# Masked row maxima of an attention kernel: the unused sums go to a byte tile instead of back into PSUM

## The chip, the cores and the metric

The kernel runs on one core of a Trainium2 chip. The time is the device time of one execution in microseconds; before and after are compared by the median of several runs. One further execution was profiled, and all rows quoted are from that one.

A core has five engines with a queue of instructions each. TensorE (PE) multiplies matrices into PSUM, which is divided into banks of 128 x 512 floats; VectorE (DVE), ScalarE (ACT) and GpSimd (POOL) work on elements; SyncE (SP) issues most DMAs. An engine takes its instructions in order; where one waits for a semaphore, all that stand behind it on the queue wait too.

## The reference

Four layers with a residual: a linear attention with learned features (A), an attention over segments with a memory (B), A, B. The change lies in B. There, 2048 tokens of 512 features are cut into 4 segments of 512 tokens, and each of 32 heads of width 16 does a causal softmax inside its segment:

```python
for s in range(N):
    qs, ks, vs = q[:, :, s], k[:, :, s], v[:, :, s]
    logits = jnp.einsum("bhqd,bhkd->bhqk", qs, ks) * scale + mask
    p = _softmax(logits, axis=-1)
    a_dot = jnp.einsum("bhqk,bhkd->bhqd", p, vs)
    pq = phi(qs)
    num = jnp.einsum("bhld,bhde->bhle", pq, M)
    den = jnp.einsum("bhld,bhd->bhl", pq, z)[..., None] + 1e-6
    a_mem = num / den
    o = g * a_mem + (1.0 - g) * a_dot
    outs.append(o)
    pk = phi(ks)
    M = M + jnp.einsum("bhld,bhle->bhde", pk, vs)
    z = z + jnp.einsum("bhld->bhd", pk)
```

A softmax subtracts the maximum of each row of logits. These row maxima are what the changed instructions compute.

## The kernel before

A layer B goes over 32 items m: 4 segments times 4 groups of heads times 2 halves, four heads an item. An item takes five steps (R = 5) of one loop in `steps`, numbered k; a table written by hand (`FIRST`, `GAPS`, `LAST`, `FINAL`) says what else each step does. Each step of the loop issues, in this order, a part of `attend(m)`, a part of `maxima` for an item some steps ahead, and the work of the table.

`maxima(m)` computes the masked row maxima. PE multiplies blocks of queries (block i, 128 rows) with the keys up to that block, 128 (i + 1) columns, for two heads at a time (e = 0, 1), the first into PSUM bank mx, the second into bank my; there is one buffer of each. The list of rounds is such that a bank holds either one product of 512 columns, or two: 128 and 384 columns, or 256 and 256. So five rounds an item, three of them with two products in a bank. Then DVE takes each product's maxima in `top`: it adds the mask to the product, takes the maximum along the row into a column of the small tile mxs, and writes the masked sums, which nobody reads, back over the product. In the profile one such maximum is two instructions: CUSTOM_DVE_ANT_0, called a pass here, and DVE_READ_ACCUMULATOR2_ANT, which delivers the maximum. PE may fill a bank again when DVE's last read is done.

`put_maxima` has PE transpose the 16 columns, ACT copy them negated into the tile mt (MT buffers), and a DMA on ACT's queue put them as a row into the stacked queries, so that the next product for `attend` subtracts the maximum by itself. `attend(m)` multiplies the same blocks into the banks lg, ACT takes the exponential of all into a tile P, POOL sets the masked triangle to zero, and `weighted` multiplies P with the values into pv.

`close` and `read` call `invert`, which turns denominators around by DMA: `compact` loads them from den into the tile dn on SP's queue, `flip` takes the reciprocal on DVE one or two steps later, `put` stores dn as inv, `spread` copies it out wide, `load` brings that back. There are two buffers of dn; the tile holds 128 x 64 floats.

The order of the work on each engine is fixed: the wrapper `Ordered` and the function `held` tie each instruction of DVE, ACT, POOL, SP and PE behind the one that the code issued before it. What a framework adds are the waits: a semaphore wait wherever an instruction touches a tile, or a bank of PSUM, that another one writes or has written, also if both are on one engine.

The helper that records an instruction has line 163 (DVE, ACT, POOL, SP) or 185 and 189 (PE's matmuls and transposes); the rows are told apart by the tiles they name.

Of the kernel before, what the change touches and what calls it, by code (L numbers as in the profile page):

```python
# [18 lines left out]
P = 128  # L19
# [8 lines left out]
OT = 3  # L28
TA = 8
OO = 5  # L30
MT = 2
PV = 1
G = 3
R = 5
# [73 lines left out]
def interleave_kernel(ctx, tc, x_in, a_wqkv, a_wphi, a_wo, b_wq, b_wk, b_wv, b_wo, b_beta,  # L108
# [4 lines left out]
    cp = ctx.enter_context(tc.tile_pool(name="cp", bufs=1))  # L113
# [10 lines left out]
    def nm(s):  # L124
        uid[0] += 1
        return f"{s}_{uid[0]}"

    def T2(tag, bufs, dt=F32, shape=(P, 512)):
        return sp.tile(list(shape), dt, tag=tag, bufs=bufs, name=nm(tag))

    def PS(tag, bufs, shape=(P, 512)):
        return ps.tile(list(shape), F32, tag=tag, bufs=bufs, name=nm(tag))
# [49 lines left out]
    def mm(*a, **k):  # L182
        n = a[0].free_size()
        work[0] += n / 2.26 if k["rhs"].dtype == F32R else (n * 2 / 2.4 + 25 if "tile_position" in k else 2 * max(112, n * 2 / 2.4))
        return held(nc.tensor.matmul(*a, **k))  # L185

    def tp(*a):
        work[0] += 108
        return held(nc.tensor.transpose(*a))  # L189
# [7 lines left out]
    mask = cp.tile([P, 512], F32, name="mask")  # L197
# [2 lines left out]
    share = cp.tile([P, 8], F32, name="share")  # L200
    gated = cp.tile([P, NC, 4], F32, name="gated")
    ones = cp.tile([32, P], F32, name="ones")

    def constants():

        sync.dma_start(out=mask, in_=c_mask)
        sync.dma_start(out=eb, in_=b_beta.unsqueeze(0).broadcast_to([P, H]))
        yield
        yield
        act.activation(eb, eb, AF.Exp, scale=-1.0)  # L210
        dve.tensor_scalar(eb, eb, 1.0, None, op0=ADD)
        dve.reciprocal(gates[:, 1, :], eb)
        dve.tensor_scalar(gates[:, 0, :], gates[:, 1, :], -1.0, 1.0, op0=MUL, op1=ADD)
        for j in range(4):
            dve.tensor_copy(share[32 * j : 32 * j + 32, :], gates[32 * j : 32 * j + 32, 0, j:H:4])
        for hf, col in enumerate((24, 28)):
            dve.tensor_scalar(share[:, hf:8:2], share[:, hf:8:2], -1.0, bd[:, col : col + 1], op0=ADD, op1=MUL)
        dve.tensor_scalar(share, share, 1.0, None, op0=ADD)
        for f in range(2):
            rows = slice(64 * f, 64 * f + 64)  # L220
            dve.tensor_tensor(out=gated[rows], op=MUL,
                              in0=gates[rows, 1, :].rearrange("p (c f h) -> p c f h", c=NC, f=2)[:, :, f, :],
                              in1=bdB[rows].unsqueeze(1).broadcast_to([64, NC, 4]))
        dve.tensor_copy(ones, bd[0:32, 25:26].broadcast_to([32, P]))
# [7 lines left out]
    def dtile(shape, name):  # L232
        return dr.tile(list(shape), F32, name=name)
# [705 lines left out]
    class LayerB:  # L939
# [98 lines left out]
        def invert(self, s, c, k, parts):  # L1038


            lo, hi = 8 * parts[0], 8 * parts[-1] + 8
            n = (hi - lo) * 4
            tiles = {}

            def compact():
                d = tiles["d"] = T2("dn", 2, shape=(P, 64))
                sync.dma_start(out=d[:, 0:n], in_=self.den(s, c)[lo:hi].rearrange("h (x i) -> (h x) i", i=n))

            def flip():
                dve.reciprocal(tiles["d"][:, 0:n], tiles["d"][:, 0:n])  # L1050

            def put():
                tiles["i"] = dtile((hi - lo, D), nm("inv"))
                sync.dma_start(out=tiles["i"].rearrange("h (x i) -> (h x) i", i=n), in_=tiles["d"][:, 0:n])

            def spread():
                wide = tiles["w"] = dtile((hi - lo, DH, D), nm("wide"))
                sync.dma_start(out=wide, in_=tiles["i"].unsqueeze(1).broadcast_to([hi - lo, DH, D]))

            def load():  # L1060
                for i in parts:
                    t = self.inv[s, c, i] = T2(*(("mmq", 2) if i else ("KN", 1)))
                    sync.dma_start(out=t, in_=tiles["w"][8 * i - lo : 8 * i - lo + 8].rearrange("h d n -> (h d) n"))
            for j, f in zip((0, 1, 2, 3, 5) if s < NSEG - 1 else (0, 2, 3, 4, 6), (compact, flip, put, spread, load)):
                self.at(k + j, f)
# [84 lines left out]
        def maxima(self, m):  # L1150


            s, c, hf = m // 8, m % 8 // 2, m % 2
            Q, K = [t[:, 2 * hf : 2 * hf + 2, :] for t in self.st[s, c]["set"]]
            mx = T2("mxs", 2, shape=(P, 16))

            def prod(pb, r, i, at, w):
                for e in range(2):
                    q, k = Q[64 * e : 64 * e + 63, r, :], K[64 * e : 64 * e + 63, r, :]
                    mm(pb[e][:, at : at + w], lhsT=q[:, i * P : (i + 1) * P], rhs=k[:, 0:w],  # L1160
                       start=True, stop=True, tile_position=(64 * e, 0))

            def top(pb, e, r, i, at):
                n = (i + 1) * P
                col = (e * 2 + r) * 4 + i
                pl = pb[e][:, at : at + n]
                with tc.high_priority():
                    dve.tensor_tensor_reduce(
                        out=pl, in0=pl, in1=mask[:, 512 - n : 512], scale=1.0, scalar=-3.0e38,
                        op0=ADD, op1=MAX, accum_out=mx[:, col : col + 1])  # L1170

            for what in ([(0, 0, 0), (0, 2, P)], [(0, 3, 0)], [(1, 0, 0), (1, 2, P)],
                         [(0, 1, 0), (1, 1, 256)], [(1, 3, 0)]):
                pb = [PS(t, 1) for t in ("mx", "my")]
                for r, i, at in what:
                    prod(pb, r, i, at, max(256, (i + 1) * P))
                for e in range(2):
                    for r, i, at in what:
                        top(pb, e, r, i, at)
                self.mx[m] = mx  # L1180
                yield

        def put_maxima(self, m):
# [3 lines left out]
            tp(pt[0:16, 0:P], self.mx.pop(m), ident)  # L1187
            mt = T2("mt", MT, F32R, shape=(16, P))
            act.activation(mt, pt[0:16, 0:P], AF.Copy, scale=-1.0)
# [352 lines left out]
```

## Time and profile before

| | us |
|---|---|
| median of 3 runs before | 1481.35 |
| lowest of them | 1480.6 |
| the profiled execution | 1477.25 |
| its span, first to last instruction | 1475.5 |
| ACT busy | 810.8 |
| POOL busy | 731.6 |
| all reads of the accumulator on DVE, 1024 | 145.1 |
| the exponentials, ACT, 320 of 128x1024 | 328.6 |

The span is what the rows of the trace cover; the 1.75 us between it and the execution's time lie around it. Busy times are of instructions that work on data; time in which an engine waits is given as idle time before an instruction, with the instruction that ended it. The rows that matter for the change are quoted in the prediction.

### The profile page before, as it was taken

To read this page: it belongs to the slowest core of one execution; us is meant where nothing else is said; L and a number is where in the kernel's file an instruction comes from. 1 tells how busy PE (TensorE), PEld (TensorE's weight loads), DVE (VectorE), ACT (ScalarE), POOL (GpSimd) and SP (SyncE) were. 2 spreads that over 40 slices of the span, in tenths; PEclk is the share of its full clock that TensorE was granted. 3 is DMA by queue.
4 is the path that set the end of the run, shared out by engine and by line. 5 is a ranking of instruction groups with operands and counts; after the bars stand their busy time and mean duration, and the time that the engine had idled before them with its cause. 6 is when DMAs were issued, how large, how long until landed. Compare 5 with 4: busy or idle time off the path is not lost.

```text
span 1475.5 us, 32962 instructions
## 1 busy us (share of the span) xinstructions
PE 1395.7 (95%) x12052; PEld 960.0 (65%) x12052; DVE 1022.0 (69%) x3007; ACT 810.8 (55%) x1228; POOL 731.6 (50%) x1066
## 2 busy tenths in 40 slices
PE   7989999999999999998899999999999999999987
PEld 6778778765566566655567887886555565566544
DVE  4766877777667767677446677867776776766762
ACT  5546345446576576565534434543656766755652
POOL 1668754224455556454424456631345556645532
PEclk9999999999999999999999999999999999999998
DMA  5387375546556556567630105764565574565451
GB/s 189 115 293 245 114 245 166 164 133 176 155 145 202 167 147 200 161 182 195 205 129 32 50 30 183 220 184 116 152 178 140 148 235 141 153 203 162 121 187 44
DMA packets 139792, 236.33 MB, mean 160 GB/s; under 512 B 26576, under 2 KB 40016, under 8 KB 138864
## 3 DMA queue, kind: packets, MB, share of 16 engines
q1 hardware_dynamic: 138480, 233.70, 52.9%
q8 instruction: 97, 1.59, 0.5%
q10 hardware_dynamic: 1152, 0.52, 0.1%
q14 instruction: 63, 0.52, 0.1%
HBM read 129.17 MB, written 55.18 MB: 125 GB/s over the span
## 4 chain that ended last, share of the span: by engine, by line
PE 73%; DVE 10%; DMA 5%; ACT 5%; issue 3%; POOL 3%; SPq 1%; ACTq 0%; POOLq 0%; DVEq 0%
PE g L185 44%; PE pv L185 8%; PE lg L185 8%; PE mx L185 4%; PE g L189 4%; PE my L185 3%; DVE mx L163 2%; ACT P L163 2%; DMA dn<-den 2%; DVE my L163 2%; PE lg L189 1%; DVE es L163 1%; SPq L163 1%; POOL tmp L163 1%; POOL P L163 1%
## 5 line engine op out<-in xcount | busy, mean ns | idle before, releaser
L163 ACT ACTIVATE P<-lg 128x1024 f32<-128x1024 f32 x320 | 328.6, 1027 | 182.3 <-PE lg L185 168.9
L163 POOL TENSOR_SCALAR_AFFINE_SELECT P<-P 128x256 f32<-128x256 f32 (+1 forms) x448 | 190.2, 439 | 427.9 <-ACT P L163 421.6
L163 DVE CUSTOM_DVE_ANT_0 mx<-mx,mask 128x128 f32<-128x128 f32 (+3 forms) x512 | 254.8, 498 | 181.7 <-PE my L185 128.7
L163 DVE CUSTOM_DVE_ANT_0 my<-my,mask 128x128 f32<-128x128 f32 (+3 forms) x512 | 265.8, 519 | 6.5
L185 PE MATMUL lg<-e,e 64*128 64x256 f32 (+2 forms) x1024 | 170.5, 391 | 26.2 <-ACT P L163 26.1
L185 PE MATMUL g<-hh,wqk 128*128 128x512 f32 x512 | 185.0, 410 | 0.7 <-ACT mt L163 0.7
L185 PE MATMUL g<-w,oh 128*128 128x512 f32 x512 | 173.4, 420 | 2.4 <-ACT oh L163 2.4
L185 PE MATMUL pv<-P,v 128*32 128x512 f32 (+3 forms) x2048 | 168.4, 448 | 2.2 <-ACT ot L163 2.2
L185 PEld LDWEIGHTS lg<-e,e 64*128 64x128 f32 x1024 | 82.1, 186 | 126.5 <-issue 55.9
L185 PE MATMUL my<-e,e 63*128 63x256 f32 (+2 forms) x512 | 148.3, 350 | 12.5 <-DVE mxs L163 11.9
L185 PE MATMUL mx<-e,e 63*128 63x256 f32 (+2 forms) x512 | 146.6, 337 | 5.9 <-DVE mxs L163 5.8
L163 DVE DVE_READ_ACCUMULATOR2_ANT mxs<- 128x1 f32 x1024 | 145.1, 142 | 0.0
L185 PE MATMUL g<-w,hh 128*128 128x512 f32 x448 | 144.8, 404 | 0.0
L185 PEld LDWEIGHTS pv<-P,v 128*32 128x32 f32 x2048 | 54.5, 110 | 105.3 <-issue 92.4
L185 PEld LDWEIGHTS g<-hh,wqk 128*128 128x128 f32 x512 | 96.6, 189 | 31.6 <-issue 10.1
L185 PEld LDWEIGHTS g<-w,oh 128*128 128x128 f32 x512 | 90.7, 193 | 30.3 <-issue 11.0
L185 PEld LDWEIGHTS my<-e,e 63*128 63x128 f32 x512 | 84.6, 187 | 32.4 <-DVE mxs L163 11.2
L185 PE MATMUL g<-w,ol 128*128 128x512 f32 x256 | 103.9, 406 | 0.0
L185 PEld LDWEIGHTS mx<-e,e 63*128 63x128 f32 x512 | 90.7, 188 | 15.4 <-DVE mxs L163 5.1
L185 PE MATMUL g<-hl,wqk 128*128 128x512 f32 x256 | 100.6, 393 | 0.0
L185 PEld LDWEIGHTS g<-w,hh 128*128 128x128 f32 x448 | 81.6, 191 | 22.7 <-issue 6.1
L163 POOL TENSOR_TENSOR P<-P,es 128x512 f32<-128x512 f32 x32 | 49.0, 1531 | 85.9 <-DVE es L163 85.8
(156 smaller groups left out, 2682.7 us busy)
## 6 DMA issues: line engine op xcount, KB each, us to landing
e<-ta SPq DMA_DIRECT2D x384, 128.0 KB
wqk<-wqk SPq DMA_DIRECT2D x64, 512.0 KB
x<-x SPq DMA_DIRECT2D x48, 256.0 KB
wide<-inv SPq DMA_DIRECT2D x20, 512.0 KB
xr<-x SPq DMA_DIRECT2D x32, 256.0 KB
x<-xr SPq DMA_DIRECT2D x28, 256.0 KB
tmp<-U SPq DMA_DIRECT2D x56, 128.0 KB
KN<-wide SPq DMA_DIRECT2D x28, 256.0 KB
```

What stands on the lines that cost most here:

```text
L163: i = f(*a, **k)
L185: return held(nc.tensor.matmul(*a, **k))
L189: return held(nc.tensor.transpose(*a))
```

## The change

In rounds with two products in a bank the masked sums go to a new tile in SBUF, junk, of bytes: two slots of 384, slot 0 for the first product and slot 1 for the second, the same two for both banks. In rounds with one product they still go back into the bank. To keep SBUF's use as it was, mt (512 bytes a partition) and dn (256 bytes) go from two buffers to one: 768 bytes, as many as junk takes.

```diff
-MT = 2
+MT = 1
...
+    junk = cp.tile([P, 2, 384], mybir.dt.uint8, name="junk")
...
             def compact():
-                d = tiles["d"] = T2("dn", 2, shape=(P, 64))
+                d = tiles["d"] = T2("dn", 1, shape=(P, 64))
...
-            def top(pb, e, r, i, at):
+            def top(pb, e, r, i, at, spare):
                 n = (i + 1) * P
                 col = (e * 2 + r) * 4 + i
                 pl = pb[e][:, at : at + n]
                 with tc.high_priority():
                     dve.tensor_tensor_reduce(
-                        out=pl, in0=pl, in1=mask[:, 512 - n : 512], scale=1.0, scalar=-3.0e38,
+                        out=pl if spare is None else junk[:, spare, 0:n], in0=pl, in1=mask[:, 512 - n : 512], scale=1.0, scalar=-3.0e38,
                         op0=ADD, op1=MAX, accum_out=mx[:, col : col + 1])
...
                 for e in range(2):
-                    for r, i, at in what:
-                        top(pb, e, r, i, at)
+                    for j, (r, i, at) in enumerate(what):
+                        top(pb, e, r, i, at, j if len(what) > 1 else None)
```

## The prediction, made before the changed kernel ran

> **What bounds the kernel now.** I read the page's first part and the chain that ended last first, for the engine that sets the time.
>
> ```profile
> PE 1395.7 (95%) x12052; PEld 960.0 (65%) x12052; DVE 1022.0 (69%) x3007; ACT 810.8 (55%) x1228; POOL 731.6 (50%) x1066
> PE 73%; DVE 10%; DMA 5%; ACT 5%; issue 3%; POOL 3%; SPq 1%; ACTq 0%; POOLq 0%; DVEq 0%
> ```
>
> TensorE (PE) is busy for 95% of the span and holds 73% of the chain; VectorE (DVE), whose work is changed, holds 10%. Next, the view of busy times by stage, for 285 to 690 us and 1003 to 1400 us, in which the attention of the two layers runs steadily (x is a count):
>
> ```profile
> core 0: us, PE busy (x) PEld busy (x) DVE busy (x) ACT busy (x) POOL busy (x), PEclk, DMA share, GB/s
> sum 802.00, PE 769.62 PEld 475.80 DVE 580.44 ACT 498.42 POOL 404.03; mean PE 384.81 PEld 237.90 DVE 290.22 ACT 249.21 POOL 202.01
> ```
>
> In these 802 us PE idles for 802.00 - 769.62 = 32.4 us and DVE works 72% of the time. So no relief of DVE there can bring more than about 32 us, 2.2% of the span. What DVE itself costs PE is in the view of the column of maxima (mxs), under who waited for it:
>
> ```profile
> who waited for it (us, times):
>   PE my L185: 11.9, 29
> ...
>   PE mx L185: 5.8, 5
> ```
>
> 34 waits, 17.7 us: matmuls into the two shared banks that DVE had not yet released.
>
> **The change part by part.** *The wait between two maxima of one bank.* One round of four maxima in order of time, DVE's rows alone (start, duration, what):
>
> ```profile
> 1207.61 0.30 DVE L163 CUSTOM_DVE_ANT_0 mx<-mx,mask 128x128 f32<-128x128 f32 x1 [0.58 <-PE mx L185]
> 1207.83 0.14 DVE L163 DVE_READ_ACCUMULATOR2_ANT mxs<- 128x1 f32 x1
> 1208.00 0.57 DVE L163 CUSTOM_DVE_ANT_0 mx<-mx,mask 128x384 f32<-128x384 f32 x1
> 1208.49 0.14 DVE L163 DVE_READ_ACCUMULATOR2_ANT mxs<- 128x1 f32 x1
> 1208.49 0.33 DVE L163 CUSTOM_DVE_ANT_0 my<-my,mask 128x128 f32<-128x128 f32 x1
> 1208.73 0.14 DVE L163 DVE_READ_ACCUMULATOR2_ANT mxs<- 128x1 f32 x1
> 1208.91 0.57 DVE L163 CUSTOM_DVE_ANT_0 my<-my,mask 128x384 f32<-128x384 f32 x1
> 1209.39 0.14 DVE L163 DVE_READ_ACCUMULATOR2_ANT mxs<- 128x1 f32 x1
> ```
>
> Each maximum is a pass (CUSTOM) and a read of its accumulator. Where the bank changes, at 1208.49, the next pass starts together with the read. Where the bank stays, it starts 0.03 us after the read has ended (1208.00 against 1207.83 + 0.14), since it reads a bank that the first pass wrote. So the wait costs 0.39 - 0.22 = 0.17 us on mx and 0.42 - 0.24 = 0.18 on my. With sums going elsewhere, that dependence is gone. But a pass that starts under a read is longer, by the shapes kept apart:
>
> ```profile
> L163 DVE CUSTOM_DVE_ANT_0 my<-my,mask 128x256 f32<-128x256 f32 x128 | 57.5, 449 | 2.2
> L163 DVE CUSTOM_DVE_ANT_0 mx<-mx,mask 128x256 f32<-128x256 f32 x128 | 55.2, 431 | 42.7 <-PE my L185 27.3 <-PE mx L185 13.0
> L163 DVE CUSTOM_DVE_ANT_0 my<-my,mask 128x128 f32<-128x128 f32 x128 | 42.4, 331 | 0.0
> L163 DVE CUSTOM_DVE_ANT_0 mx<-mx,mask 128x128 f32<-128x128 f32 x128 | 37.9, 296 | 60.6 <-PE my L185 40.1 <-PE mx L185 19.5
> ```
>
> my at 128x128 always follows another bank's pass, mx mostly follows a pause: 331 against 296 ns, 0.03 us that the released pass pays. Net 0.14 us a pair. Pairs: the 256 passes of 128x128 each go with one of 128x384, the 256 of 128x256 go with each other, 128 pairs; 384 in all, 384 x 0.14 = 54 us of DVE time.
>
> On DVE's queue the 34 ns and the read are idle time of an engine that mostly has slack, so the path decides. By the 29 waits for my: one shared round holds two waits, 0.28 us of relief, and the mean wait is 11.9 / 29 = 0.41 us, so 29 x 0.28 = 8.1 us come back. One of them:
>
> ```profile
> 1166.81 0.57 DVE L163 CUSTOM_DVE_ANT_0 my<-my,mask 128x384 f32<-128x384 f32 x1
> 1167.29 0.14 DVE L163 DVE_READ_ACCUMULATOR2_ANT mxs<- 128x1 f32 x1
> 1167.58 0.35 PE L185 MATMUL my<-e,e 63*128 63x256 f32 x1 [0.54 <-DVE mxs L163]
> ```
>
> The five waits for mx hold the late DMA below, so I count nothing for them. By the chain instead: its shares are "DVE mx 2.1%" and "DVE my 1.6%", 3.7% of 1475.5 = 55 us, while all passes are busy for 254.8 + 265.8 = 520.6 us:
>
> ```profile
> by line: PE g L185 43.8%; PE pv L185 8.2%; PE lg L185 7.6%; PE mx L185 4.4%; PE g L189 3.7%; issue 3.3%; PE my L185 3.1%; DVE mx L163 2.1%; ACT P L163 1.8%; DMA dn<-den 1.8%; DVE my L163 1.6%; PE lg L189 1.4%; DVE es L163 1.2%; SPq L163 1.1
> L163 DVE CUSTOM_DVE_ANT_0 mx<-mx,mask 128x128 f32<-128x128 f32 (+3 forms) x512 | 254.8, 498 | 181.7 <-PE my L185 128.7
> L163 DVE CUSTOM_DVE_ANT_0 my<-my,mask 128x128 f32<-128x128 f32 (+3 forms) x512 | 265.8, 519 | 6.5
> ```
>
> A tenth of the passes lies on it, so a tenth of 54 us, 5.7. I take 8, between 5.7 and all 17.7.
>
> The Trainium skill speaks against part of this: "VectorE: DVE Perf Modes", section Terms, has a pipeline flush after every op, before whose end the next op can't issue. By that, a released pass would start at the first one's end, 0.30 us after its start, and gain 0.09 a pair, some 5 us on the path. The trace does not agree: at 1208.49 the pass on my starts 0.08 us before the pass on mx ends (1208.00 + 0.57).
>
> *The output as bytes in SBUF.* No row of before stores bytes, so I bound it. Below: the nearest row with PSUM and SBUF in and SBUF out, and the pass of the same size:
>
> ```profile
> L163 DVE TENSOR_TENSOR ta<-g,ta 128x512 fp32r<-128x512 f32 x64 | 44.1, 689 | 43.6 <-ACT ta L163 25.6 <-ACT tb L163 18.0
> L163 DVE CUSTOM_DVE_ANT_0 mx<-mx,mask 128x512 f32<-128x512 f32 x128 | 89.2, 697 | 74.1 <-PE my L185 61.2 <-PE mx L185 11.9
> ```
>
> 8 ns less a pass at the best, 768 x 8 ns = 6 us of DVE, a tenth of it on the path: 0.6. At the worst bytes go at half rate (a rival below). I take nothing, by the row above, which is the nearest. "Perfetto Trace Analysis" of the Trainium skill, section Optimizing Scalar/DVE Operations, puts the access overhead at about 60 ns on SBUF and 125 on PSUM; were it the output's place that sets it, four passes of a late round would gain 0.26 us more, another 7 us on the path; the 8 ns speak against it.
>
> *New order among bytes.* The small tile has two slots, so a pass must follow the one two before it. In the round above the fourth pass would wait for the read at 1208.49, which ends at 1208.63; with 0.03 us of signalling it may start at 1208.66, and the third pass frees the engine only at 1208.73. In the built program 142 more wait instructions stand in DVE's queue, ahead of third and first passes, for work of two passes before; they pass while the preceding pass runs. Nothing, or, if the fourth pass did wait as long as now, half of the 8 us. The order of instructions on every engine is otherwise the same.
>
> *One buffer for the negated maxima (mt).* ScalarE's copy must now wait until the last one's DMA has been read out.
>
> ```profile
> 1203.02 0.53 ACTq L163 DMA_DIRECT2D e<-mt  x1
> 1216.56 0.25 ACT L163 ACTIVATE mt<-g 16x128 fp32r<-16x128 f32 x1
> ```
>
> 13.5 us lie between, and the slow store below lands in 6.0. Nothing; behind a wait there the next exponentials would queue.
>
> *One buffer for the compact denominators (dn).* In four places the next load follows the last store directly on SP's queue; it now waits for that store to land, and all that SP issues later waits behind it. The dear one and a cheap one:
>
> ```profile
> 683.55 0.81 SPq L163 DMA_DIRECT2D inv<-dn  x1
> 684.40 0.43 SPq L163 DMA_DIRECT2D dn<-den  x1
> 685.63 0.32 SPq L163 DMA_DIRECT2D x<-xr  x1
> 689.59 0.57 SPq L163 DMA_DIRECT2D wide<-inv  x1
> 689.81 0.35 DVE L163 RECIPROCAL dn<-dn 128x32 f32<-128x32 f32 x1 [2.82 <-DMA dn<-den]
> ...
> 1396.84 0.38 SPq L163 DMA_DIRECT2D inv<-dn  x1
> 1397.32 0.39 SPq L163 DMA_DIRECT2D dn<-den  x1
> 1403.32 0.35 DVE L163 RECIPROCAL dn<-dn 128x32 f32<-128x32 f32 x1
> ```
>
> And from the chain in order of time (start, length), such a load elsewhere:
>
> ```profile
> 373.67 1.64 DMA dn<-den
> ```
>
> The store of 683.55 lands only just before 689.59, when the copy of its result (wide) starts, after 6.0 us. So the load of 684.40 moves to about 689.6; with the 1.64 us of the other it lands at 691.2, 1.5 us after the landing that now lets DVE go at 689.81. DVE idles for it already, and PE behind DVE. I charge 1.5 us; 0 if the queue lets PE catch up, 6 if the load is as slow there as the store before it. At 1397.32 there are 6 us until the reciprocal: free. The other two places look like it.
>
> Sum, on the profiled execution: 1477.25 us (span 1475.5 and 1.75 around it) - 8 + 1.5 = 1470.8, 0.44% less. That execution lies 4.1 us under the runs' median of 1481.35; the same share of the median gives **1475 us**.
>
> **The rivals.** *PE is given nothing back (0.20).* A freed PE runs into ScalarE's exponentials, for which it waits already:
>
> ```profile
> PE lg L185 <- ACT P L163: 26.1, 31, 3.8
> ```
>
> 31 waits, 26.1 us; each relief ahead of one of them lengthens it. Against it: the two banks are filled after lg in the same step, so part stays. With the 1.5 us of dn: 1480 to 1483.
>
> *Slower: bytes are stored at half rate (0.07).* From 128x128 to 128x256 a pass on mx grows by 431 - 296 = 135 ns; half rate adds as much for each 128 columns, 0.27 us a pass at the mean of 256, over 768 passes 207 us. A shared round gets 4 x 0.27 - 0.28 = 0.8 us longer. The 29 late rounds pay 0.8 each, 23 us, and if half of the 192 shared rounds become late, 77: 1504 to 1558, say 1530. It decides from 0.07 us a pass, where a round is no shorter than now. For it: no byte output is in the trace; against it: the type of the SBUF output above (fp32r) costs nothing.
>
> *Faster: DVE gates ScalarE too (0.06).* If an earlier DVE also moved the casts and exponentials behind it, most of the 32.4 us of PE's idle time would go: 1481 - 30 = 1451. Against it: the 26.1 us above wait on exponentials that wait on PE's own products.
>
> *The change doesn't release the pass (0.07).* The bytes' own order holds it, or the start under a read costs more than 0.03 us: 1481 to 1484.
>
> **How the numbers follow.** My forecast, a gain of 3 to 18 us, has 0.60. A measurement of this kernel can tell about 2% from no change, 30 us. The forecast, no gain and no release all lie within it; of the fast case half reaches past it. Faster 0.03, slower 0.07, the same 0.90. The range runs from a gain of 18 us (1463) to what the cases of no gain give with 6 us for dn in place of 1.5: 1486.
>
> **What would show it.** In the profile after, on DVE: the 128x384 pass on mx starts with the read before it, 0.22 us after the first pass, and its mean grows from 566 to about 600 ns; no pass is otherwise longer. PE's waits on mxs for my fall from 11.9 to about 4 us. The load of dn near 684 starts after its store lands. I am wrong if a 128x256 pass grows by over 70 ns, if the released pass still starts 0.17 us late, or if PE's waits on P grow by what those on mxs lose.

## The result, and the profile after

| | before | after |
|---|---|---|
| median, us | 1481.96 (1480.6 to 1843.29, 4 runs) | 1465.97 (1465.39 to 1466.08, 4 runs) |
| ratio | | 0.9894 [0.9875, 0.9914] |
| profiled execution, us | 1477.25 | 1465.91 |
| its span, us | 1475.5 | 1464.2 |

One run before took 1843.29 us; the ratio leaves it out, and without it the median before is 1481.35. So the change makes the kernel 15.4 us faster by the medians, 1.06% by the ratio. That is less than the 2% from which a difference is counted as told, but the interval lies clear of 1. The prediction had 1475 us, a gain of 0.43%: the direction was right, the gain two and a half times as large. The question is where the other 9 to 10 us came from.

The page of the kernel after, its busy times and its chain by engine:

```profile
PE 1382.4 (94%) x12052; PEld 952.9 (65%) x12052; DVE 954.3 (65%) x3007; ACT 809.2 (55%) x1228; POOL 731.6 (50%) x1066
...
PE 69%; DVE 9%; DMA 7%; ACT 7%; issue 3%; POOL 3%; SPq 1%; ACTq 0%; POOLq 0%; DVEq 0%
```

DVE's busy time falls by 67.7 us. But PE's *busy* time falls as well, by 13.3 us, with the same 12052 matmuls. The span is only 11.3 us shorter, so PE's idle time has not shrunk at all: it has grown by 2.0 us. That is the surprise of this case.

DVE's rows of one round of four maxima after (start, duration, what), of the same shapes as the round that the prediction shows, and the instruction behind it:

```profile
1202.56 0.29 DVE L163 CUSTOM_DVE_ANT_0 junk<-mx,mask 128x128 uint8<-128x128 f32 x1 [0.54 <-PE mx L185]
1202.78 0.08 DVE L163 DVE_READ_ACCUMULATOR2_ANT mxs<- 128x1 f32 x1
1202.78 0.55 DVE L163 CUSTOM_DVE_ANT_0 junk<-mx,mask 128x384 uint8<-128x384 f32 x1
1203.26 0.08 DVE L163 DVE_READ_ACCUMULATOR2_ANT mxs<- 128x1 f32 x1
1203.26 0.29 DVE L163 CUSTOM_DVE_ANT_0 junk<-my,mask 128x128 uint8<-128x128 f32 x1
1203.47 0.08 DVE L163 DVE_READ_ACCUMULATOR2_ANT mxs<- 128x1 f32 x1
1203.47 0.55 DVE L163 CUSTOM_DVE_ANT_0 junk<-my,mask 128x384 uint8<-128x384 f32 x1
1203.94 0.08 DVE L163 DVE_READ_ACCUMULATOR2_ANT mxs<- 128x1 f32 x1
```

Every pass now starts with the read of the pass before it, also inside a bank (1202.78, 1203.47). From the first pass to the end of the last read it takes 1203.94 + 0.08 - 1202.56 = 1.46 us; before it took 1209.39 + 0.14 - 1207.61 = 1.92. PE may fill my 0.46 us earlier, not 0.28 as forecast. The groups by shape (total us, mean ns) show why, first after, then the read before:

```profile
L163 DVE DVE_READ_ACCUMULATOR2_ANT mxs<- 128x1 f32 x1024 | 100.0, 98 | 0.0
...
L163 DVE CUSTOM_DVE_ANT_0 junk<-mx,mask 128x384 uint8<-128x384 f32 x128 | 70.7, 553 | 0.0
...
L163 DVE CUSTOM_DVE_ANT_0 junk<-my,mask 128x128 uint8<-128x128 f32 x128 | 36.6, 286 | 0.0
L163 DVE CUSTOM_DVE_ANT_0 junk<-mx,mask 128x128 uint8<-128x128 f32 x128 | 36.5, 285 | 63.1 <-PE my L185 38.6 <-PE mx L185 23.6
```

```profile
L163 DVE DVE_READ_ACCUMULATOR2_ANT mxs<- 128x1 f32 x1024 | 145.1, 142 | 0.0
```

The released pass of 384 columns did not grow from 566 to 600 ns, it takes 553. The pass on my at 128 columns, which started under a read before too, fell from 331 to 286. And a read behind a pass that writes SBUF takes 0.08 us, not 0.14.

Who waited for the maxima in mxs, after (us, times), and how long PE waited for the exponentials:

```profile
who waited for it (us, times):
...
  PE mx L185: 11.0, 5
...
  PE my L185: 2.7, 12
```

```profile
PE lg L185 <- ACT P L163: 31.1, 36, 3.8
```

PE's waits for my fell by 9.2 us as forecast. Those for mx rose by 5.2 and those for the exponentials by 5.0. Counted by idle time, the change brought nothing.

**Where the gain is.** The stretch around one such wait, before and after, with PE's and DVE's rows:

```profile
1204.57 0.40 PE L185 MATMUL mx<-e,e 63*128 63x512 f32 x1
...
1204.83 0.14 DVE L163 DVE_READ_ACCUMULATOR2_ANT mxs<- 128x1 f32 x1
...
1205.11 0.46 PE L185 MATMUL my<-e,e 63*128 63x512 f32 x1
1205.51 1.28 PE L185 MATMUL pv<-P,v 128*32 128x384 f32 x16
...
1207.12 0.28 PE L185 MATMUL mx<-e,e 63*128 63x256 f32 x1
1207.13 0.34 PE L185 MATMUL my<-e,e 63*128 63x256 f32 x1
```

```profile
1199.82 0.08 DVE L163 DVE_READ_ACCUMULATOR2_ANT mxs<- 128x1 f32 x1
...
1199.93 0.39 PE L185 MATMUL mx<-e,e 63*128 63x512 f32 x1
1200.05 0.47 PE L185 MATMUL my<-e,e 63*128 63x512 f32 x1
...
1200.45 1.28 PE L185 MATMUL pv<-P,v 128*32 128x384 f32 x16
```

The products for mx and my use different halves of the array (63 rows each) and run side by side when both banks are free: 1207.12 and 1207.13. At 1204.57 only mx was free. DVE's last read on my ended at 1204.97, the product for my started at 1205.11, and what follows (pv) started 0.94 us after the product for mx. After the change the read ends before mx even starts, and pv follows after 0.52 us. 0.42 us are gained, although PE was idle for only 0.14 us of the wait before (1204.97 to 1205.11); during the rest of it, it counted as busy with half of the array.

So I divided PE's time in each trace: every stretch belongs to the matmul whose end lies past all earlier ones ("alone"), every gap to the matmul that ends it ("idle"). The time before PE's first matmul and after its last one is left out. Where two matmuls start at the same instant, the order of the trace decides which of them is "alone"; this can move up to 1.7 us between the columns mx alone and my alone, and leaves their sum as it is. The products into mx and my, 512 each, in us:

| kernel (all described below) | mx alone | mx idle | my alone | my idle | sum | other idle |
|---|---|---|---|---|---|---|
| before | 76.4 | 5.9 | 47.9 | 12.5 | 142.8 | 48.1 |
| after | 77.7 | 11.0 | 35.3 | 3.8 | 127.7 | 53.4 |
| single | 77.8 | 9.5 | 47.5 | 12.3 | 147.2 | 46.8 |
| bybank | 75.8 | 8.8 | 40.9 | 7.3 | 132.9 | 50.1 |
| first | 77.0 | 9.1 | 41.9 | 9.2 | 137.1 | 50.0 |
| inter | 79.7 | 10.3 | 37.5 | 3.7 | 131.3 | 52.7 |
| full | 77.4 | 6.3 | 34.4 | 4.3 | 122.4 | 54.8 |
| all | 80.0 | 10.5 | 28.8 | 3.6 | 122.9 | 54.9 |
| short | 79.5 | 9.3 | 14.2 | 0.0 | 103.0 | 54.7 |
| swap | 109.1 | 32.7 | 8.0 | 0.0 | 149.7 | 47.5 |

From before to after: my idle -8.7, **my alone -12.6**, mx idle +5.1, mx alone +1.3, other idle +5.3, all other work -2.0. That is -11.6, and the spans differ by 11.3. Each line of the table is one profiled execution, and these differ in PE's granted clock too (0.985 before, 0.986 after, 0.980 in inter); the gains below are therefore taken from the ratios, and the table says only where in PE's time they lie.

### The profile page after: what moved, and what is told of

Its sections match the earlier page's. It is cut to its first block, busy times and chain, and to the rows that moved or that the text cites. A ratio compares the mean times of both kernels' runs of the same rounds, so it can differ in the third digit from the quotient of the medians.

```text
span 1464.2 us, 33119 instructions
## 1 busy us (share of the span) xinstructions
PE 1382.4 (94%) x12052; PEld 952.9 (65%) x12052; DVE 954.3 (65%) x3007; ACT 809.2 (55%) x1228; POOL 731.6 (50%) x1066
## 4 chain that ended last, share of the span: by engine, by line
PE 69%; DVE 9%; DMA 7%; ACT 7%; issue 3%; POOL 3%; SPq 1%; ACTq 0%; POOLq 0%; DVEq 0%
PE g L185 43%; PE lg L185 7%; PE pv L185 7%; PE mx L185 4%; PE g L189 3%; ACT P L163 3%; PE my L185 2%; DMA inv<-dn 1%; PE lg L189 1%; DVE es L163 1%; POOL tmp L163 1%; DVE junk L163 1%; POOL P L163 1%; SPq L163 1%; DMA dn<-den 1%
## 5 line engine op out<-in xcount | busy, mean ns | idle before, releaser
L163 DVE CUSTOM_DVE_ANT_0 junk<-mx,mask 128x128 uint8<-128x128 f32 (+2 forms) x384 | 146.7, 420 | 124.6 <-PE my L185 87.8
L163 DVE CUSTOM_DVE_ANT_0 mx<-mx,mask 128x512 f32<-128x512 f32 x128 | 89.0, 696 | 104.5 <-PE my L185 82.2
L163 DVE CUSTOM_DVE_ANT_0 junk<-my,mask 128x128 uint8<-128x128 f32 (+2 forms) x384 | 146.7, 419 | 0.0
L185 PEld LDWEIGHTS g<-hh,wqk 128*128 128x128 f32 x512 | 97.0, 190 | 31.8 <-issue 11.3
L163 DVE DVE_READ_ACCUMULATOR2_ANT mxs<- 128x1 f32 x1024 | 100.0, 98 | 0.0
```

The costliest lines, as they stand in the source:

```text
L163: i = f(*a, **k)
```

## The experiments

All ratios are to the kernel before, on the same chip, with their 95% interval; a gain in us is the ratio's on some 1480 us. My theory: two things shorten a round, the released wait and the sums' place in SBUF, and PE gains what hidden waits it loses.

**The wait alone (inter).** Edit of the kernel before; the sums go back into PSUM:

```diff
-                for e in range(2):
-                    for r, i, at in what:
+                for r, i, at in what:
+                    for e in range(2):
                         top(pb, e, r, i, at)
```

> The kernel before with one edit: the passes alternate between the banks, first product of mx, first of my, second of mx, second of my; sums still go back into the bank. A pass that follows one on the other bank starts under its read, as at 1208.49 us of the trace of before, so that the wait should go without any new tile. By the theory that the round's length decides, a round of 128 and 384 columns should take 1.43 to 1.47 us in place of 1.785 (passes at their lengths of before, reads of 141 ns), some 60 us of DVE less, the lag of my behind mx should fall from 49.6 to about 35 us, and the time by 0.5 to 0.8%: ratio 0.992 to 0.995. By the rival that what is gained comes from where the sums go (shorter reads and passes), the ratio stays at 0.998 to 1.002.

Measured: 1467.78 us, ratio 0.9919 [0.9893, 0.9944], a gain of 12.0 us (8.3 to 15.8). A round of its trace, first and last rows, and two groups by shape:

```profile
1207.32 0.30 DVE L163 CUSTOM_DVE_ANT_0 mx<-mx,mask 128x128 f32<-128x128 f32 x1 [0.57 <-PE mx L185]
...
1207.79 0.60 DVE L163 CUSTOM_DVE_ANT_0 mx<-mx,mask 128x384 f32<-128x384 f32 x1
1208.30 0.14 DVE L163 DVE_READ_ACCUMULATOR2_ANT mxs<- 128x1 f32 x1
1208.30 0.60 DVE L163 CUSTOM_DVE_ANT_0 my<-my,mask 128x384 f32<-128x384 f32 x1
1208.82 0.14 DVE L163 DVE_READ_ACCUMULATOR2_ANT mxs<- 128x1 f32 x1
```

```profile
L163 DVE CUSTOM_DVE_ANT_0 mx<-mx,mask 128x384 f32<-128x384 f32 x128 | 76.5, 598 | 0.0
...
L163 DVE CUSTOM_DVE_ANT_0 mx<-mx,mask 128x128 f32<-128x128 f32 x128 | 37.9, 296 | 60.3 <-PE my L185 38.0 <-PE mx L185 21.2
```

1208.82 + 0.14 - 1207.32 = 1.64 us: 0.28 less than before, the relief that I had forecast for a round, and here the pass that starts under a read does grow from 566 to 598 ns. So this kernel tries the forecast's own relief. The table says where it lands: my idle falls by 8.8 us, which is the 8 of the forecast, and my alone by a further 10.4, which the forecast had not counted. Part of it is taken back: mx idle is 4.4 longer, other idle 4.6 and mx alone 3.3. This one execution is only 0.7 us shorter in span than the one before, at its lower clock; the 12.0 us are those of twelve runs. The rival, that only the sums' place counts, falls.

**The place of the sums alone (bybank).** Edit of the changed kernel; the slot goes by bank, so that two passes of a bank write the same slot and wait as before:

```diff
-                        top(pb, e, r, i, at, j if len(what) > 1 else None)
+                        top(pb, e, r, i, at, e if len(what) > 1 else None)
```

> The changed kernel, but the slot goes by the bank: both products of a bank write into the same slot, so that the second pass of a bank waits for the read of the first one as in the kernel before, while the sums still go to SBUF as bytes. Theory R (the gain is the wait that went): no gain, 1480 to 1484 us, all of the lead gone. Theory S (the shorter passes and reads, 83 ns a read in place of 141 in the profile after, bring their part): a shared round takes 327 + 478 + 327 + 478 ns = 1.61 us against 1.785 before and 1.376 after, 43% of the relief: 1473 to 1477 us.

Measured: 1468.84 us, 0.9954 [0.9933, 0.9975], a gain of 6.8 us. In this comparison the kernel before took 1475.94 us, and the times expected here and for first were worked out from some 1481; on 1481 the ratio gives 1474.2, which is theory S. A round:

```profile
1205.01 0.29 DVE L163 CUSTOM_DVE_ANT_0 junk<-mx,mask 128x128 uint8<-128x128 f32 x1 [0.53 <-PE mx L185]
1205.23 0.08 DVE L163 DVE_READ_ACCUMULATOR2_ANT mxs<- 128x1 f32 x1
1205.34 0.56 DVE L163 CUSTOM_DVE_ANT_0 junk<-mx,mask 128x384 uint8<-128x384 f32 x1
...
1206.64 0.08 DVE L163 DVE_READ_ACCUMULATOR2_ANT mxs<- 128x1 f32 x1
```

The second pass starts 0.03 us after the read's end (1205.23 + 0.08), so the wait is there, but the round takes 1.71 us, 0.21 less than before. The edit that I had costed at nothing is worth 7 us by itself, with the single buffers of mt and dn still in. Three of the four reads lie on the round's length, and 3 x 59 ns = 0.18 us of the 0.21 is theirs.

**Only the first product to bytes (first).**

```diff
-                        out=pl if spare is None else junk[:, spare, 0:n], in0=pl, in1=mask[:, 512 - n : 512], scale=1.0, scalar=-3.0e38,
+                        out=pl if spare != 0 else junk[:, spare, 0:n], in0=pl, in1=mask[:, 512 - n : 512], scale=1.0, scalar=-3.0e38,
```

> The changed kernel, but only the first product of a bank writes to the byte tile; the second one writes back over itself. The second pass is released as in the changed kernel, while half of the shared passes write to PSUM. Theory R (the released wait makes the gain): 1466 to 1470 us, almost all of it. Theory S (the place of the output makes half of it or more): 1472 to 1476 us. In the profile a read after a pass that writes PSUM takes 0.14 us and one after a pass that writes bytes 0.08, and the pass that starts under a 0.14 us read is 0.03 us longer.

Measured: 1469.02 us, 0.9949 [0.9925, 0.9973], which on 1481 us is 1473.4. The second pass still starts 0.03 us after the first one's read, now behind a read of 0.08 us:

```profile
1210.32 0.29 DVE L163 CUSTOM_DVE_ANT_0 junk<-mx,mask 128x128 uint8<-128x128 f32 x1 [0.59 <-PE mx L185]
1210.54 0.08 DVE L163 DVE_READ_ACCUMULATOR2_ANT mxs<- 128x1 f32 x1
1210.65 0.57 DVE L163 CUSTOM_DVE_ANT_0 mx<-mx,mask 128x384 f32<-128x384 f32 x1
```

The second pass here writes the bank that the first one reads, and that is enough to keep the wait. The premise of my expectation fell; the run is a second one with the wait kept, beside bybank, and agrees with it.

**The other bank last (swap).** Edit of the kernel before:

```diff
-                for e in range(2):
+                for e in (1, 0):
                     for r, i, at in what:
                         top(pb, e, r, i, at)
```

> The kernel before with one edit: in each round DVE takes the maxima of my first and those of mx after it. The work, the waits between two passes of a bank and the length of a round stay as they are; only the bank that comes free last changes. By the theory of the hidden wait, PE lost as much before by starting the products for my behind those for mx, without being idle, as it would lose by waiting openly: the time should stay within 0.3% of before, the 49.6 us by which the products for my start after those for mx (all 512 pairs) should be nearly gone or turn negative, PE's busy time should fall by some 30 us from 1395.7, and PE's idle waits for mx on the maxima should rise from 5.8 us to some 40 to 50. By the theory of the prediction, where only idle waits count, the number and length of these waits stay as they were, some 18 us in all for both banks, and PE's busy time stays near 1396.

Measured: 1482.96 us, 1.0011 [0.9984, 1.0037]: no difference. Who waited for the maxima, and the stages of the prediction's second view:

```profile
  PE mx L185: 30.9, 54
```

```profile
sum 802.00, PE 759.62 PEld 462.16 DVE 580.53 ACT 496.64 POOL 403.21; mean PE 379.81 PEld 231.08 DVE 290.27 ACT 248.32 POOL 201.60
```

With the same work in a time that can't be told apart, PE's idle time on the maxima is 30.9 us where it was 17.7, and PE's busy time in these 802 us is 10.0 us less. Now mx is the late bank, PE takes mx first, and the wait is an open one. That is a part of the hidden wait of the kernel before, made visible. The sizes were smaller than I expected (30.9 against 40 to 50 us, and 7.5 us less busy time over the whole span, 1395.7 to 1388.2, against some 30), for mx alone rose by 32.7 us where my alone fell by 39.9: side by side, the first of the two products is the one that the account books.

**Nearly no passes (short).** Edit of the kernel before; each pass covers 16 columns, without the causal mask, so the maxima of all other columns are left out:

```diff
-                n = (i + 1) * P
+                n = 16
...
-                        out=pl, in0=pl, in1=mask[:, 512 - n : 512], scale=1.0, scalar=-3.0e38,
+                        out=pl, in0=pl, in1=mask[:, 0:n], scale=1.0, scalar=-3.0e38,
```

> The kernel before with every pass cut to the first 16 columns of its product, unmasked: the maxima are left out for the rest, so that the output is not the reference's, and DVE's passes cost next to nothing, while the wait between two passes of a bank stays. It bounds what DVE's passes cost the time. A shared round falls from 1.785 us to about 0.75, a single one from 1.27 to 0.25: some 330 us less of DVE. Theory D (only the waits that PE has on DVE can be won, 17.7 us in the trace of before): 0.985 to 0.99, no better than the changed kernel by more than 5 us. Theory G (a fifth of DVE's relief goes on reaching the time, through the casts and DMAs that queue behind the passes too): 0.96 to 0.975.

Measured: 1444.89 us, 0.9775 [0.9739, 0.9811], a gain of 33.3 us. The page:

```profile
PE 1364.8 (95%) x12052; PEld 942.4 (65%) x12052; DVE 708.1 (49%) x3007; ACT 807.9 (56%) x1228; POOL 732.7 (51%) x1066
```

314 us less of DVE bring 33. PE's busy time falls by 30.9 us with all its matmuls in place, and my alone by 33.7. The ratio of 0.9775 lies between what my two theories gave (0.985 to 0.99, and 0.96 to 0.975). The reads and the waits between two passes of a bank are still in this kernel, so 33 us is near the most that quicker maxima can bring here, but no strict bound; the change has a little under half of it.

**The single buffers alone (single), and the change without them (full).** Single is the kernel before with the first edit; full is the changed kernel with that edit undone:

```diff
-MT = 2
+MT = 1
...
-                d = tiles["d"] = T2("dn", 2, shape=(P, 64))
+                d = tiles["d"] = T2("dn", 1, shape=(P, 64))
```

> The kernel before with one buffer of mt and one of dn, and nothing else changed: what the two single buffers cost by themselves. Theory A (from the trace after: between the exponential at 688.75 us and the one at 695.62 us the changed kernel loses 4.95 us of its lead, where the load of dn waits for the store before it to land): 1.5 to 5 us slower than before, ratio 1.001 to 1.004, the loss at that one place, in the first layer B. Rival B (PE catches up behind it, so that the loss was only lead that the next wait for a DMA would have taken anyway): within 1 us of before.

> The changed kernel with two buffers of mt and two of dn again; the byte tile stays (SBUF has room for it). Theory A (the single buffers cost 1.5 to 5 us on the path): 1461 to 1464.5 us where the changed kernel has 1466. Rival B (they cost nothing): 1465 to 1467. In the profile the load of dn follows the store at once again.

Measured: single 1479.38 us, 1.0018 [0.9998, 1.0037]; full 1462.77 us, 0.9906 [0.9877, 0.9935]. SP's rows in single, and ACT's exponentials around the place, first before, then single:

```profile
681.35 1.44 SPq L163 DMA_DIRECT2D inv<-dn  x1
687.31 0.32 SPq L163 DMA_DIRECT2D dn<-den  x1
```

```profile
688.75 1.02 ACT L163 ACTIVATE P<-lg 128x1024 f32<-128x1024 f32 x1 [1.32 <-PE lg L185]
...
695.62 1.02 ACT L163 ACTIVATE P<-lg 128x1024 f32<-128x1024 f32 x1 [3.04 <-PE lg L185]
```

```profile
686.57 1.02 ACT L163 ACTIVATE P<-lg 128x1024 f32<-128x1024 f32 x1 [1.31 <-PE lg L185]
...
697.01 1.02 ACT L163 ACTIVATE P<-lg 128x1024 f32<-128x1024 f32 x1 [4.70 <-PE lg L185]
```

The load moved as predicted, 5.96 us behind the store instead of 0.85. Between the two exponentials lie 10.44 us in place of 6.87: 3.6 us lost here, not 1.5. PE's rows divide it. The wait for mx at this place grows from 2.21 to 3.69 us, which is the 1.5 that I charged. Behind it the same twelve products into g take 4.76 us (691.66 to 696.42) in place of 3.00 (692.03 to 695.03): the granted clock is 0.50 from 690 to 694 us in single, and 1.00 from 691 to 695 before. What lowers the clock was not tested; it is 0.50 from 690 to 694 us in full as well, which has two buffers. Over the run single is 2.7 us slower (-0.3 to +5.5), which does not exclude that the single buffers cost nothing. In the changed kernel the account does not settle it either: mx idle is 11.0 us with the single buffers and 6.3 in full, but 10.5 in the run all (below), which has two buffers too. The ratios of full (0.9906) and of the changed kernel (0.9894, 0.9914 and 0.990 in three comparisons) don't tell the two apart.

**Another type (bf16), all passes (all, all2), and the change once more (again, again2).** Again and again2 are the changed kernel as it is. Edits of it for bf16, and for all, which has two buffers of mt and dn too:

```diff
-    junk = cp.tile([P, 2, 384], mybir.dt.uint8, name="junk")
+    junk = cp.tile([P, 2, 384], mybir.dt.bfloat16, name="junk")
```

```diff
-    junk = cp.tile([P, 2, 384], mybir.dt.uint8, name="junk")
+    junk = cp.tile([P, 2, 512], mybir.dt.uint8, name="junk")
...
-                        top(pb, e, r, i, at, j if len(what) > 1 else None)
+                        top(pb, e, r, i, at, j if len(what) > 1 else e)
```

> The changed kernel with the spare tile in bf16 in place of bytes (1536 bytes a partition; SBUF has the room). Theory P (passes and reads are shorter because the output isn't in PSUM): the same 83 ns a read and 284, 420 and 553 ns a pass, and the time of the changed kernel. Theory B (because bytes are stored): the read goes back to 0.14 us or the pass to 296, 431 and 566 ns, and part of the gain goes, ratio 0.991 to 0.995.

> The changed kernel itself once more, on the chip of the three others of this call, so that they can be held against it. Ratio to before 0.988 to 0.992.

> Every pass, also the one of 512 columns, writes to the byte tile (two slots of 512), and mt and dn have two buffers. A version that could beat both. A round of one product a bank then saves the 0.03 us of the pass that starts under a long read and some 0.013 us a pass, 0.06 us; 128 such rounds, 7 us of DVE. At the share of DVE's relief that reached the time so far (7 of 30 us for the two kernels that kept the wait, 16 of 78 for the changed one, about a fifth) 1.5 us less than with two buffers alone: ratio 0.987 to 0.991. If rounds of one product are never late: equal to the kernel with two buffers, 0.9906.

> All passes to bytes in SBUF, with two buffers of mt and dn, once more, beside the changed kernel on one chip. By the lag theory it is 0.2 to 0.4% below the changed kernel: 3 to 6 us, of which up to 2 are for dn. If the 512-column passes and dn are worth nothing, both give the same time.

> The changed kernel once more, for the comparison on one chip with the three others: ratio to before 0.988 to 0.993, as in its two earlier comparisons.

| kernel | median us | ratio |
|---|---|---|
| bf16 | 1463.19 | 0.9899 [0.9864, 0.9935] |
| again | 1467.03 | 0.9914 [0.988, 0.9948] |
| all | 1461.04 | 0.9868 [0.9828, 0.9908] |
| again2 | 1464.33 | 0.990 [0.987, 0.993] |
| all2 | 1460.7 | 0.9877 [0.9846, 0.9907] |

The type doesn't matter: the 128x384 pass into bf16 takes as long as into bytes.

```profile
L163 DVE CUSTOM_DVE_ANT_0 junk<-mx,mask 128x384 bf16<-128x384 f32 x128 | 70.7, 553 | 0.0
```

In the run all the same two effects appear where there was no wait to remove:

```profile
L163 DVE CUSTOM_DVE_ANT_0 junk<-my,mask 128x512 uint8<-128x512 f32 x128 | 87.8, 686 | 0.0
L163 DVE DVE_READ_ACCUMULATOR2_ANT mxs<- 128x1 f32 x1024 | 85.0, 83 | 0.0
```

The 512-column pass on my falls from 730 to 686 ns, and all reads now take 83. It is 6.0 and 3.6 us below the changed kernel in the two comparisons that had both on one chip (again and all, again2 and all2), and my alone falls by another 6.5 us (by 5.6 against full, which has two buffers of mt and dn as well). The intervals overlap, so of the kernels that compute all maxima it is the fastest by its medians, and not shown to be faster than the changed one.

## Why the prediction was right in direction and wrong in size

**The wait between two maxima of one bank: right.** The released pass starts with the read before it, 0.22 us after the first pass (1202.78). The trace again does not agree with the flush rule of the Trainium skill's "VectorE: DVE Perf Modes", section Terms, if the end of a pass in the profile is the end of its flush: that pass starts 0.07 us before the first one's end (1202.56 + 0.29).

**"I take 8, between 5.7 and all 17.7": wrong, and the main failure.** The step took the relief on the path from PE's idle waits alone, 29 waits for my. These came back as forecast (my idle -8.7). But a wait for my is at first hidden behind the product for mx, which runs on half of the array, and this time counts as busy. That part, my alone, gave 12.6 us more. Inter shows it at the forecast's own relief: -8.8 idle and -10.4 alone, and by the ratio a gain of 12.0 us (8.3 to 15.8) instead of 8. Swap shows that at least a part of this time is a wait: change the bank that is late, and PE's busy time falls by 7.5 us over the span while the kernel's time stays as it was. For the same reason the first bound, "no relief of DVE there can bring more than about 32 us", does not hold as it was reasoned: short gains 33.3 us over the whole run while PE's busy time falls by 30.9 and its idle time (two columns idle and the last one) only from 66.5 to 64.0.

**"The output as bytes in SBUF ... I take nothing": wrong, the second failure.** The row of 689 ns (ta) was right about the pass itself: 8 ns less by that row, 11 measured (697 to 686 in the run all). But ta has no accumulator, so that row could not show the two things that changed more: the read (142 to 83 ns), and the 32 to 35 ns that a pass pays under a read when it writes PSUM. Bybank, where the sums' place and the single buffers differ from before, gains 6.8 us (3.7 to 9.9). The rule that I had weighed and set aside, about 60 ns of access on SBUF and 125 on PSUM ("Perfetto Trace Analysis" of the Trainium skill, section Optimizing Scalar/DVE Operations), would have added another 7 us by my estimate; the reads of 142 and 83 ns differ by about as much, the free passes of 697 and 686 ns do not.

**"0.03 us that the released pass pays": wrong for this output.** It pays when the sums go to PSUM (inter, 598 ns), not when they go to SBUF (553). The place decides and not the shorter read: in first the 128-column pass on my starts under a read of 0.14 us, writes SBUF, and takes 286 ns. With the shorter reads, a round's relief was 0.46 us and not 0.28.

**The new order among bytes: right.** The fourth pass starts with the third's read (1203.47); DVE's wait instructions cost nothing that shows.

**dn: the place and the mechanism right, the price low.** 3.6 us in single's trace where I charged 1.5, within the 0 to 6 of the prediction. The longer wait is the 1.5; the rest is mostly the lower clock behind it, which I had not counted. The three other places and mt are not told apart from nothing.

**The rivals.** "PE is given nothing back" was right on idle time: the 9.2 us that the waits for my lost came back as 5.2 for mx and 5.0 for the exponentials. My sign for being wrong, that PE's waits on P grow by what those on mxs lose, thus came up (5.0 against 4.0), and yet the kernel was faster, as the gain was in busy time. Bytes at half rate fell (553 ns, bf16 the same), and so did the rival without a release (1202.78). That DVE gates ScalarE too had 1451 us, far below the 1466 measured.

**The range held by luck.** The measured 1465.97 us lies inside 1463 to 1486, but its lower end is a gain of 18 us, as much as all 17.7 us of idle waits, and the gain did not come from there: idle time as a whole did not fall.

Summed by single runs: inter's -12.0 and bybank's -6.8, which carries the single buffers, give -18.8, against -12.7 to -15.7 by the ratios of the three comparisons of the change. In a round the two reliefs nearly add up (0.28 + 0.21 us, together 0.46), but not over the run: my alone and my idle together fall by 12.2 us in bybank, 19.2 in inter and 21.3 in the change, so the second relief finds little left to win. The intervals of inter and of the change overlap; that the bytes bring more on top of the released wait is not shown.

## What to carry to other kernels

An engine that runs two instructions side by side can wait and still be booked as busy: compare when the partners start, or change which one is late, before the idle time is taken as the bound. Results that nobody reads need not go back where they came from; where they go sets both which waits remain and how long the instruction takes. The release of the wait could be had without a new tile, by alternating between the banks (inter).

## What was not expected of the hardware

- The accumulator's read takes 142 ns behind a pass that writes PSUM and 83 behind one that writes SBUF, whatever the type of the sums (bytes or bf16).
- A pass of masked maxima that starts under such a read is longer by 32 to 35 ns when it writes PSUM (566 to 598, 296 to 331), and not longer when it writes SBUF (in first, at 128 columns, 286 under a read of 142 ns and 284 mostly behind a pause).
- Two matmuls of 63 rows on different halves of the array that start together (1207.12 and 1207.13) take 0.28 and 0.34 us; after a late start of the second one (1204.57 and 1205.11) they take their times one after the other, with no idle time of PE before the second but the last 0.14 us.
